# A hand-ordered attention and FFN kernel: the work of the first two blocks put in another order, q and k of the first pair loaded in halves by two queues

## The chip, the cores and the metric

One core of a Trainium2 chip. The time is the device time of one execution in microseconds (us). An interval of three runs stands beside the median where there is one.

## What is computed

Eight batches ("blocks" here) of linear attention with 8 heads, 576 rows and 64 columns each, and then one FFN over all 4608 rows, in float32:

```python
q_s = exp(q - max(q, axis=-1)); q_s = q_s / (sum(q_s, axis=-1) + 1e-9)      # per row
k_s = exp(k - max(k, axis=2));  k_s = k_s / (sum(k_s, axis=2) + 1e-9)       # per column, over 576 rows
kv  = einsum('bhsd,bhse->bhde', k_s, v)
x   = einsum('bhsd,bhde->bhse', q_s, kv)  ->  (4608, 512)
out = (relu(x @ w_in) ** 2) @ w_out       # w_in 512x2048, w_out 2048x512
```

## The kernel before, in words

**Tiles.** The eight heads of a block are taken as four pairs (`pr` 0 to 3); a pair fills 128 partitions. 512 of the 576 rows of a block go through the FFN directly, the other 64 ("left") are kept in DRAM for later. The FFN of a block has 16 steps `n` (128 of the 2048 hidden columns each). A step has four parts `h{n}_{c}`, where `c` is the pair whose x it multiplies, then `relu`, `rm` (times itself), `ghi` and `glo` (split in a rounded high part and the rest), and four parts `o{n}_{t}` into four output banks. Each part is three TensorE matmuls of 128x512, since each float32 product is made of high times high, high times low and low times high.

**A pair.** For q: `qm` (row maxima, DVE), `qsub` (POOL), `qexp` (ACT), `qs` (sums, DVE), `qadd` (POOL), `rc` (reciprocal, DVE), `qmul` (POOL), then `qt4` and `qt1` (transposes on TensorE) and `cp`, `cps` (copies by ACT). For k: `kmax` (DVE), `T` (transpose on TensorE), `mc` (DVE), `spread` (TensorE), `ke` (subtract, DVE), `kexp` (ACT), `kv` (TensorE, needs v as well), `rs`, `rr` (DVE), `kvn` (ACT or DVE). Then `at` (TensorE, x of 512 rows), `xhi` (ACT), `xlo` (DVE), and `atl`, `left`, `XL` for the 64 rows. A name with two digits, `kmax03`, is block 0, pair 3.

**Weights.** Each 128-column chunk `i{n}` of w_in and each chunk `o{n}` of w_out comes raw in 512 KB (`Li0`, `Lo0`), and is turned into a high and a low part by seven units: `L` (transfer), `low`, `t` (ACT), `s1`, `s2` (DVE), `hi` (ACT), `lo` (POOL). This is done once, beside the first block.

**What sets the order.** `ORDER` (line 51) is a list of these units, written out; the loop at line 1237 calls them one by one. The class `InOrder` (line 279) chains every instruction of an engine to the one before it on that engine, so each of TensorE, DVE, ACT, POOL and the transfer queue SP works through the list in its order and stops at the first unit whose input is late. A number behind a colon is the TensorE bank. `Z3:2` is three filler matmuls into bank 2; at the very start `beat(BEATS, banks[0])` (line 395) puts 28 fillers on TensorE, in front of everything. `ORDER` covers blocks 0 and 1 of the attention, the conversion of all weights, the 16 FFN steps of block 0 and the first two of block 1 (n = 16, 17), and parts of block 2; from `LIST` (line 91) on another list is followed, which stays as it is.

**Loads.** `load(b, pr, n)` (line 401) brings k, q or v of a pair in two transfers, the lower 64 partitions (160 KB) and the upper 64 (128 KB), on SP. Two exceptions stand at line 406 and 410: `Lk00` brings the lower half of k on SP and the unit `Lk00b` the upper half on ACT's queue; `Lq00` brings both halves of q on ACT's queue. The unit `warm` is a tiny exponential on ACT, there to get ACT's function table loaded early. Two tiles `kt` and `qt` serve the even and odd pairs of block 1 and later, so `Lk10` writes the tile that `kmax00` and `ke00` read.

Of the kernel before, what the change touches and what calls it, by code (L numbers as in the profile page):

```python
# [66 lines left out]
o3_0 o3_1 o3_2 relu4 Lv12 qexp11 kmax20 kexp12 Lq12 XL01 relu5 XL02 s1i6 s2i6 hii6 loi6 h6_0:1 h6_1 h6_2 h6_3 Lk13
rm4 qs11 qadd11 to4 s1o4 s2o4 Lo5 ghi4 hio4 glo4 loo4 o4_3 o4_2 o4_0 o4_1 atl10:0 Li8 qm12 qsub12 ti7 rm5 ghi5
kv12:3 glo5 lowo5 s1i7 s2i7 hii7 loi7 kmax13 relu6 rm6 h7_0:1 to5 s1o5 lowi8 s2o5 qexp12 qs12 qadd12 h7_1 h7_2 h7_3
rc11 qmul11 left10 T13:0 hio5 ti8 s1i8 Lo6 lowo6 rs12 rr12 kvn12 s2i8 to6 s1o6 qt411:3 Li9 loo5 o5_0 Lv11 o5_1 relu7  # L70
rm7 s2o6 hii8 loi8 o5_3 kv11:1 mc13 ghi6 glo6 ti9 cp11 lowi9 Lo7 lowo7 spread13 hio6 loo6 h8_0:3 h8_1 h8_2 Li10 ke20
rs11 rr11 kvn11 s1i9 s2i9 rc12 qmul12 Lo8 lowo8 at11:1 Li13 Lo10 ke13 to7 s1o7 s2o7 hii9 xhi11 lowi10 o6_3 loi9
xlo11 qt111:0 cps11 ti10 s1i10 s2i10 o5_2 ghi7 lowo10 glo7 o6_0 atl11:0 left11 Li15 hio7 loo7 to8 s1o8 s2o8 Lo11
hii10 h8_3 relu8 o6_2 hio8 rm8 h9_0:1 h9_1 h9_2 h9_3 relu9 o6_1 Lk21 o7_3 lowi15 qt412:0 ghi8 Li11 lowi11 kmax21
kexp13 loo8 loi10 o7_0 cp12 ti11 s1i11 s2i11 rm9 qt112:3 cps12 Lo9 o7_1 Lq13 qm13 lowo9 to9 hii11 o7_2 s1o9 glo8
o8_3 Lo13 at12:0 xhi12 h10_0:3 h10_1 h10_2 h10_3 XL11 Lv13 loi11 h11_0:1 h11_1 xlo12 kv13:0 h11_2 ghi9 glo9 Lq20
h11_3 qsub13 lowo11 relu10 Lo14 Li14 s2o9 ti12 hio9 loo9 o9_3 o8_1 o9_1 rm10 atl12:3 qexp13 s1i12 s2i12 to10 s1o10
s2o10 hii12 loi12 relu11 Lo12 Lv20 lowi13 qs13 qadd13 ti13 kexp20 lowi14 Lo15 Lq21 o8_0 o9_0 s1i13 hio10 loo10 rs13
rr13 kvn13 s2i13 rm11 lowo14 Lv21 WA0 WA1 ko0 ko1 to11 o8_2 o9_2 ghi10 ghi11 h12_0:0 h12_1 h12_2 h12_3 rc13 qmul13
s1o11 s2o11 ti14 s1i14 qsub20 Lq22 hio11 lowo12 qt413:1 left12 XL10 glo10 o10_2 o10_3 Lk22 hii13 relu12 qt113:3  # L80
o10_1 lowo13 cps13 atl13:3 left13 XL13 rm12 kv20:0 s2i14 loo11 XL12 loi13 h13_0:3 h13_1 h13_2 h13_3 hii14 qexp20
# [1255 lines left out]
```

## Time and profile before

| | us |
|---|---|
| median of 3 runs (838.13 to 839.73) | 838.84 |
| the profiled execution's own time | 838.89 |
| its span in the trace | 837.1 |
| TensorE busy (matmuls) | 828.8 (99%) |
| DVE busy | 540.8 (65%) |
| ACT busy | 486.7 (58%) |
| POOL busy | 288.2 (34%) |

The span is what lies between the first and the last instruction; 1.8 us of the profiled execution lie around it. Matmuls are pipelined, so that a busy TensorE is not one that does useful work all the time: the fillers count as busy, and so does a matmul that stands in the pipeline while the next one waits. All instructions have line 290, since one helper issues them; they are told apart by the tiles they write and read. Times of day below are us from the start of the span.

### The profile page before, as it was taken

To read this page: it belongs to the slowest core of one execution; us is meant where nothing else is said; L and a number is where in the kernel's file an instruction comes from. 1 tells how busy PE (TensorE), PEld (TensorE's weight loads), DVE (VectorE), ACT (ScalarE), POOL (GpSimd) and SP (SyncE) were. 2 spreads that over 40 slices of the span, in tenths; PEclk is the share of its full clock that TensorE was granted. 3 is DMA by queue.
4 is the path that set the end of the run, shared out by engine and by line. 5 is a ranking of instruction groups with operands and counts; after the bars stand their busy time and mean duration, and the time that the engine had idled before them with its cause. 6 is when DMAs were issued, how large, how long until landed. Compare 5 with 4: busy or idle time off the path is not lost.

```text
span 837.1 us, 12969 instructions
## 1 busy us (share of the span) xinstructions
PE 828.8 (99%) x4286; PEld 678.2 (81%) x4286; DVE 540.8 (65%) x1098; ACT 486.7 (58%) x898; POOL 288.2 (34%) x269
## 2 busy tenths in 40 slices
...
GB/s 240 270 186 299 279 287 214 327 215 98 211 256 249 227 283 259 277 281 258 234 252 245 283 159 213 271 187 189 172 233 177 98 227 156 163 166 154 186 55 50
DMA packets 156594, 179.65 MB, mean 215 GB/s; under 512 B 51696, under 2 KB 120304, under 8 KB 156528
## 3 DMA queue, kind: packets, MB, share of 16 engines
...
## 4 chain that ended last, share of the span: by engine, by line
PE 90%; DVE 4%; DMA 2%; issue 1%; POOL 1%; ACT 1%; SPq 1%; DVEq 0%; POOLq 0%; ACTq 0%
PE bank L290 90%; DVE m L290 1%; DMA raw_o<-in_moe_w_out_dram 1%; DMA qt<-in_q_dram 1%; SPq L290 1%; DMA raw_i<-in_moe_w_in_dram 0%; POOL qs L290 0%; DVE qs L290 0%; DVE g_lo L290 0%; DVE w L290 0%; POOL qn L290 0%; DVE xf L290 0%; DVE bank L290 0%; DVE r L290 0%; DVE qm L290 0%
## 5 line engine op out<-in xcount | busy, mean ns | idle before, releaser
L290 PE MATMUL bank<-wp,g 128*128 128x512 f32 x648 | 160.7, 390 | 0.0
L290 PEld LDWEIGHTS bank<-wp,g 128*128 128x128 f32 x648 | 120.6, 188 | 24.9
L290 PE MATMUL bank<-x_hi,wi 128*128 128x512 f32 x384 | 131.3, 396 | 0.0
L290 PE MATMUL bank<-xh_T,wp 128*128 128x512 f32 x384 | 130.7, 390 | 0.0
L290 PE MATMUL bank<-wo,g_hi 128*128 128x512 f32 x384 | 120.3, 394 | 0.0
L290 PE MATMUL bank<-xh_B,wp 128*128 128x512 f32 x288 | 98.0, 390 | 0.0
L290 POOL TENSOR_TENSOR qs<-qT,qs 64x640 fp32r<-64x640 f32 (+1 forms) x40 | 64.2, 1604 | 94.4 <-ACT qs L290 63.1
L290 DVE TENSOR_TENSOR c<-c,bank 128x512 f32<-128x512 f32 x48 | 32.9, 686 | 86.7 <-ACT c L290 86.4
L290 PEld LDWEIGHTS bank<-xh_T,wp 128*128 128x128 f32 x384 | 72.1, 188 | 16.3 <-ACT bank L290 1.2
L290 PEld LDWEIGHTS bank<-x_hi,wi 128*128 128x128 f32 x384 | 72.2, 188 | 15.9 <-DVE x_lo L290 0.4
L290 ACT ACTIVATE far<-far 128x512 f32<-128x512 f32 x96 | 60.6, 632 | 41.1 <-DVE far L290 39.9
L290 PEld LDWEIGHTS bank<-wo,g_hi 128*128 128x128 f32 x384 | 70.5, 188 | 14.8 <-ACT g_hi L290 0.4
L290 PE MATMUL bank<-wo,g_lo 128*128 128x512 f32 x192 | 75.0, 391 | 0.0
L290 PE MATMUL bank<-x_lo,wi 128*128 128x512 f32 x192 | 74.9, 390 | 0.0
L290 PE MATMUL bank<-xl_T,wp 128*128 128x512 f32 x192 | 74.8, 389 | 0.0
L290 PE MATMUL bank<-wo_back,g 128*128 128x512 f32 x288 | 71.4, 389 | 0.0
L290 DVE TENSOR_TENSOR g<-far,g 128x512 fp32r<-128x512 f32 x48 | 35.7, 781 | 43.5 <-ACT g L290 43.4
L290 DVE TENSOR_TENSOR far<-far,bank 128x512 f32<-128x512 f32 x48 | 32.9, 685 | 47.7 <-PE bank L290 47.5
L290 PEld LDWEIGHTS bank<-xh_B,wp 128*128 128x128 f32 x288 | 54.1, 188 | 11.6
L290 PEld LDWEIGHTS bank<-wo_back,g 128*128 128x128 f32 x288 | 53.6, 188 | 11.0
L290 POOL TENSOR_TENSOR qn<-qn,qs 128x640 f32<-128x640 f32 x30 | 37.8, 1261 | 69.6 <-DVE qs L290 47.0
L290 ACT CAST g<-far 128x512 fp32r<-128x512 f32 x48 | 27.5, 619 | 49.7 <-PE bank L290 49.4
...
## 6 DMA issues: line engine op xcount, KB each, us to landing
...
out_dram<-o SPq DMA_DIRECT2D x68, 128.0 KB, 2.9
...
```

What stands on the lines that cost most here:

```text
L290: ins = f(*args, **kwargs)
```

## The change

Two things. In `load`, q and k of block 0, pair 0 are both brought in halves: the lower on SP (`Lq00`, `Lk00`), the upper on ACT's queue (new unit `Lq00b`, and `Lk00b` as before). And `ORDER` is another arrangement of the same units (732 before, the one new unit besides), with the same banks and the same fillers; q of pairs 0 and 1 comes first, `Lk00b` now stands behind `warm`, and v of pair 1 comes before k of pair 2. `LIST` and all units stay the same.

```diff
 ORDER = """
-Lk00 Lq00 Lk00b warm qm00 qsub00 Lq01 qexp00 qm01 kmax00 qs00 Lk01 Li0 kmax01 T01:0 qsub01 qexp01 qadd00 rc00 Lk02
-Lq02 qs01 qadd01 Lq03 T00:1 mc00 mc01 Z3:2 spread01 rc01 kmax02 ti0 lowi0 s1i0 Li1 Lv01 ke01 kexp01 Z4:2 T02:2
-qmul01 qt101:3 Lk03 qm02 spread00 qt401:4 cps01 mc02 Lv00 qm03 Li2 qmul00 qt400:5 cp00 qt100:6 Z5:0 kv01:0 s2i0 ti1
-Lv02 ke00 Lk10 cps00 spread02 qsub03 qexp03 kmax03 lowi1 qsub02 qexp02 Z3:3 T03:3 qs03 rs01 rr01 kexp00 mc03 Lv03
-Li3 cp01 Z3:5 kv00:5 Lq10 spread03 kvn01 at01:1 atl01:6 qadd03 rc03 qmul03 qt403:4 lowi2 qs02 qadd02 rs00 rr00 kvn00
-ke02 kexp02 rc02 qmul02 hii0 cp03 atl00:0 ke03 kexp03 s1i1 s2i1 ti2 padv00 kmax10 qt103:5 cps03 at00:2 Lo0 hii1 loi1
-kv02:3 rs02 rr02 kvn02 xhi00 qt402:4 kv03:5 cp02 at02:3 Li4 T10:4 s1i2 xlo00 xhi01 rs03 rr03 kvn03 h1_0:2 xlo01
-xhi02 loi0 mc10 s2i2 at03:1 left00 lowi3 Lo1 qm10 ti3 xlo02 xhi03 lowo0 qt102:5 hii2 Lk11 Lv10 qsub10 s1i3 s2i3 hii3
...
-kvn10 hii4 lowo2 spread11 ke11 h3_3 to2 at10:2 loi4 h4_0:0 Li12 ghi0 kmax12 qt110:6 hio0 left02 T12:4 mc12 relu3
...
-h15_0:3 h15_1 h15_2 h15_3 Lv22 WA2 WA3 ko2 ko3 ghi13 relu14 to14 s1o14 s2o14 to15 glo13 o13_3 o13_1 o13_2 hio14
-loo14 o13_0 s1o15 s2o15 hio15 rm14 ghi14 glo14 h16_0:1 relu15 rm15 ghi15 glo15 Bw20 Lk23 WA4 ko4 o14_3 qsub21 at13:3
-loo15 o15_3 xhi13 xlo13 o14_0 o15_0 B20 rs20 h16_1 rr20 qexp21 ev3 S3 qn21 ev0 S0 ko6 Bw21 h16_2 o14_1 o15_1 ev1
...
+Lq00 Lq00b Lq01 warm Lk00 Lk00b Lk01 Lv01 qm01 Lk02 qsub01 qm00 Li0 qexp01 kmax00 qsub00 Li1 Lq03 kmax01 qexp00 Lq02
+qs01 T01:0 T00:1 Z3:2 mc01 qadd01 qs00 Lk03 spread01 Z4:2 rc01 mc00 qadd00 ke01 qmul01 Lv00 rc00 ti0 kmax02 qmul00
+lowi0 kexp01 s1i0 T02:2 qt101:3 spread00 qt401:4 cps01 s2i0 Li2 qt400:5 mc02 ti1 qm03 Lv03 qt100:6 Z5:0 cps00 cp01
+ke00 qsub03 lowi1 Lv02 kv01:0 qm02 kexp00 kmax03 qsub02 qexp03 Lk10 spread02 Z3:3 cp00 qs03 padv01 T03:3 qexp02 Lo0
+Z3:5 mc03 qadd03 rs01 hii0 Li3 rr01 kv00:5 rc03 qs02 qmul03 kvn01 s1i1 lowi2 Lq10 spread03 at01:1 rs00 padv00 rr00
+ke02 loi0 kvn00 Li4 atl01:6 s2i1 qt403:4 kexp02 Li5 qadd02 ke03 atl00:0 qt103:5 ti2 at00:2 Lk11 rc02 kmax10 cp03
+qmul02 kv02:3 cps03 left00 kexp03 Lo1 s1i2 xhi00 qt402:4 s2i2 hii1 kv03:5 Lv10 rs02 cp02 rr02 loi1 kvn02 xhi01 xlo00
+at02:3 lowi3 rs03 rr03 xlo01 ti3 T10:4 h1_0:2 qm10 hii2 h1_1 mc10 kvn03 s1i3 loi2 spread10 xhi02 at03:1 s2i3 lowi4
+xlo02 Lo2 qt102:5 hii3 h0_0:0 qsub10 ke10 xhi03 h1_2 cps02 xlo03 kexp10 loi3 h2_0:3 Li6 lowo0 h0_1 kmax11 Lk12 to0
...
+rr10 h3_1 s2i4 late cp10 glo1 mc11 h3_2 kvn10 hii4 kmax12 h3_3 to2 loi4 left02 spread11 hio1 o0_3:5 s1o2 relu3 qt110:6
+loo1 qm11 at10:2 lowi6 ke11 lowi12 h4_0:0 qsub11 s2o2 xhi10 o1_3 kexp11 xlo10 T12:4 h4_1 hio2 mc12 rm3 spread12 ti5
...
+qexp21 glo13 h15_0:3 hio13 XL13 rm14 h15_1 to14 loo13 Lk22 kf20 ghi14 h15_2 s1o14 kh20 h15_3 s2o14 o13_1 kl20 hio14
+Lq23 o13_3 relu15 loo14 to15 o13_2 rm15 Bw20 s1o15 o13_0 XL12 at13:3 s2o15 ko4 ghi15 glo14 hio15 h16_0:1 B20 xhi13
+loo15 h16_1 glo15 o14_3 xlo13 o15_3 Lv22 h16_2 ev3 o14_1 qn21 h16_3 qh20 o15_1 ko6 o14_0 S3 relu16 ql20 o15_0 rm16
...
 """.split()
@@ -403,13 +403,12 @@
-        if (b, pr, n) == (0, 0, 0):
-            units["Lk00b"] = lambda: e.act.dma_start(dst[HALF:, :, :HIGH, :], hi)
+        if (b, pr) == (0, 0) and n < 2:
+            units[f"L{'kq'[n]}00b"] = lambda: e.act.dma_start(dst[HALF:, :, :HIGH, :], hi)
             e.sp.dma_start(dst[:HALF], lo)
         elif n < 2 or b == 0:
-            on = e.act if (b, pr, n) == (0, 0, 1) else e.sp
-            on.dma_start(dst[:HALF], lo)
-            on.dma_start(dst[HALF:, :, :HIGH, :], hi)
+            e.sp.dma_start(dst[:HALF], lo)
+            e.sp.dma_start(dst[HALF:, :, :HIGH, :], hi)
```

## Rows read from the trace of the kernel before

**Rows 1.** Page: the chain that ended last, shares by engine.
```profile
PE 90%; DVE 4%; DMA 2%; issue 1%; POOL 1%; ACT 1%; SPq 1%; DVEq 0%; POOLq 0%; ACTq 0%
```

**Rows 2.** Chain of waits in order of time: start, length, what was waited for.
```profile
46.79 80.29 PE bank L290 x426
...
127.14 0.68 DVE r L290
...
194.58 637.71 PE bank L290 x3178
```

**Rows 3.** Timeline, TensorE: start, length, operation, count; fillers, first transpose, first FFN matmul, then at03.
```profile
1.31 9.39 PE L290 MATMUL bank<-x_hi 128*128 128x512 f32 x28 [1.31 <-POOL x_hi L290]
...
11.49 0.41 PE L290 MATMUL bank<-ident,m 128*128 128x128 f32 x2 [0.80 <-DVE qs L290]
...
29.53 0.50 PE L290 MATMUL bank<-x_hi,wi 128*128 128x512 f32 x1
...
30.55 1.12 PE L290 MATMUL bank<-qe,kvn 128*128 128x512 f32 x2
```

**Rows 4.** Waits by engine, 29.5 to 138 us: TensorE's weight loads (us, times, longest).
```profile
PEld bank L290 <- DVE mc L290: 0.8, 2, 0.5
PEld bank L290 <- DVE g_lo L290: 0.7, 2, 0.4
...
PEld bank L290 <- DVE m L290: 0.5, 1, 0.5
PEld bank L290 <- DVE r L290: 0.4, 1, 0.4
PEld bank L290 <- ACT g_hi L290: 0.4, 1, 0.4
```

**Rows 5.** Timeline from the start: the first transfers on both queues, ACT and DVE.
```profile
0.73 1.41 ACTq L290 DMA_DIRECT2D qt<-in_q_dram  x2
...
1.55 1.52 SPq L290 DMA_DIRECT2D qt<-in_q_dram  x2
...
2.17 0.62 ACTq L290 DMA_DIRECT2D kt<-in_k_dram  x1
...
2.82 1.28 ACT L290 ACT_TABLE_LOAD   x1 [2.82 <-issue]
...
4.12 0.20 ACT L290 ACTIVATE mc<-ones 128x1 f32<-128x1 f32 x1
...
6.18 0.82 DVE L290 TENSOR_REDUCE qm<-qt 128x10 f32<-128x640 f32 x1 [3.25 <-DMA qt<-in_q_dram]
```

**Rows 6.** Busy time by stretch: PE, PEld, DVE, ACT, POOL, clock, DMA share, GB/s.
```profile
5.00:10.00 5.00, 5.00 (x19) 4.03 (x18) 3.46 (x4) 1.15 (x2) 2.48 (x2) 1.00 1.09 274
```

**Rows 7.** Transfers issued before 30 us: count, KB each, median us from issue to landing.
```profile
qt<-in_q_dram ACTq DMA_DIRECT2D x1, 160.0 KB, 3.1
...
kt<-in_k_dram ACTq DMA_DIRECT2D x1, 128.0 KB, 4.5
```

**Rows 8.** Groups on DVE from 5 to 29 us: count, busy us, mean ns of one, idle before.
```profile
L290 DVE TENSOR_REDUCE m<-kt 128x128 f32<-128x640 f32 x5 | 6.5, 1299 | 0.0
L290 DVE TENSOR_REDUCE qm<-qt 128x10 f32<-128x640 f32 x4 | 3.3, 814 | 3.6 <-DMA qt<-in_q_dram 3.6
L290 DVE TENSOR_TENSOR ke<-kt,bank 128x640 f32<-128x640 f32 x4 | 3.2, 796 | 0.0
```

**Rows 9.** Timeline, DVE and SP: ke00, Lk10, kmax03, rs00, rr02, s2i2 and xlo00.
```profile
17.41 0.81 DVE L290 TENSOR_TENSOR ke<-kt,bank 128x640 f32<-128x640 f32 x1
18.14 1.30 DVE L290 TENSOR_REDUCE m<-kt 128x128 f32<-128x640 f32 x1
18.25 1.25 SPq L290 DMA_DIRECT2D kt<-in_k_dram  x2
...
22.43 0.16 DVE L290 TENSOR_SCALAR rs<-bank 128x1 f32<-128x1 f32 x1 [1.00 <-PE bank L290]
...
27.24 0.16 DVE L290 RECIPROCAL rs<-rs 128x1 f32<-128x1 f32 x1 [0.28 <-DVE rs L290]
...
28.78 0.69 DVE L290 TENSOR_TENSOR x_lo<-bank,x_hi 128x512 fp32r<-128x512 f32 x1
...
30.44 0.68 DVE L290 SCALAR_TENSOR_TENSOR w<-raw_i,bank 128x512 uint32<-128x512 uint32 x1
```

**Rows 10.** Timeline, POOL: the low part of o1.
```profile
42.39 1.30 POOL L290 TENSOR_TENSOR wo<-w,wo 128x512 fp32r<-128x512 f32 x1 [1.22 <-ACT wo L290]
```

More of the change, by code (lines that the diff above doesn't have):

```diff
@@ L57 @@
-ke02 kexp02 rc02 qmul02 hii0 cp03 atl00:0 ke03 kexp03 s1i1 s2i1 ti2 padv00 kmax10 qt103:5 cps03 at00:2 Lo0 hii1 loi1
-kv02:3 rs02 rr02 kvn02 xhi00 qt402:4 kv03:5 cp02 at02:3 Li4 T10:4 s1i2 xlo00 xhi01 rs03 rr03 kvn03 h1_0:2 xlo01
-xhi02 loi0 mc10 s2i2 at03:1 left00 lowi3 Lo1 qm10 ti3 xlo02 xhi03 lowo0 qt102:5 hii2 Lk11 Lv10 qsub10 s1i3 s2i3 hii3
-xlo03 spread10 ke10 loi2 qexp10 Lo2 h0_0:0 h0_1 qs10 cps02 h1_1 h1_2 h1_3 loi3 Li5 h0_2 to0 s1o0 lowo1 h2_0:3 h2_1
-h2_2 relu1 h3_0:1 kexp10 Lk12 qadd10 rc10 qmul10 lowi4 left01 s2o0 to1 rm1 h0_3 ghi1 glo1 h2_3 kmax11 atl03:4 s1o1
@@ L62 @@
-s2o1 padv01 Lo3 ti4 s1i4 left03 hio1 atl02:5 qt410:2 kv10:6 cp10 s2i4 loo1 rs10 rr10 T11:4 h3_1 mc11 h3_2 relu0 rm0
-kvn10 hii4 lowo2 spread11 ke11 h3_3 to2 at10:2 loi4 h4_0:0 Li12 ghi0 kmax12 qt110:6 hio0 left02 T12:4 mc12 relu3
-h4_1 h4_2 h4_3 loo0 kexp11 Lq11 s1o2 spread12 s2o2 late xhi10 xlo10 lowi5 glo0 o0_3:5 o1_3 o0_0:2 o1_0 hio2 ti5 loo2
-ke12 o0_2:4 o1_2 relu2 s1i5 Li6 Lo4 s2i5 lowo3 to3 hii5 loi5 qm11 cps10 o0_1:6 o1_1 Lk20 qsub11 rm2 h5_0:3 h5_1 h5_2
-h5_3 s1o3 s2o3 XL03 lowi12 lowi6 ghi2 glo2 o2_3 o2_1 o2_2 o2_0 lowo4 rm3 ghi3 glo3 Li7 ti6 XL00 lowi7 hio3 loo3 o3_3
@@ L67 @@
[L67 to L81, printed above, removed]
@@ L87 @@
-qh20 ql20 kf20 h16_3 relu16 rm16 ghi16 S1 B21 glo16 o14_2 o15_2 ev2 S2 kh20 kl20 Lq23 h17_0:3 h17_1 h17_2 h17_3
+Lq00 Lq00b Lq01 warm Lk00 Lk00b Lk01 Lv01 qm01 Lk02 qsub01 qm00 Li0 qexp01 kmax00 qsub00 Li1 Lq03 kmax01 qexp00 Lq02
+qs01 T01:0 T00:1 Z3:2 mc01 qadd01 qs00 Lk03 spread01 Z4:2 rc01 mc00 qadd00 ke01 qmul01 Lv00 rc00 ti0 kmax02 qmul00
+lowi0 kexp01 s1i0 T02:2 qt101:3 spread00 qt401:4 cps01 s2i0 Li2 qt400:5 mc02 ti1 qm03 Lv03 qt100:6 Z5:0 cps00 cp01
+ke00 qsub03 lowi1 Lv02 kv01:0 qm02 kexp00 kmax03 qsub02 qexp03 Lk10 spread02 Z3:3 cp00 qs03 padv01 T03:3 qexp02 Lo0
@@ new lines @@
+h0_2 left01 qexp10 h0_3 s1o0 lowi5 h3_0:1 qs10 lowo1 Lq11 h2_1 s2o0 qadd10 relu0 rc10 h2_2 qmul10 to1 rm0 Li12 h1_3
+hio0 s1o1 Lo3 h2_3 ghi0 loo0 s2o1 relu1 atl03:4 atl02:5 kv10:6 ti4 rm1 glo0 left03 s1i4 lowo2 qt410:2 rs10 ghi1 T11:4
+rr10 h3_1 s2i4 late cp10 glo1 mc11 h3_2 kvn10 hii4 kmax12 h3_3 to2 loi4 left02 spread11 hio1 o0_3:5 s1o2 relu3 qt110:6
+loo1 qm11 at10:2 lowi6 ke11 lowi12 h4_0:0 qsub11 s2o2 xhi10 o1_3 kexp11 xlo10 T12:4 h4_1 hio2 mc12 rm3 spread12 ti5
+loo2 h4_2 ke12 qexp11 o0_0:2 s1i5 cps10 Lk20 kexp12 o1_0 s2i5 lowo3 o0_1:6 qs11 Lo4 to3 o1_1 XL03 hii5 qadd11 s1o3
@@ new lines @@
+o0_2:4 relu2 Lv12 loi5 s2o3 h4_3 rm2 ti6 o1_2 kmax20 ghi2 h5_0:3 hio3 glo2 h5_1 XL00 ghi3 h5_2 Li7 lowo4 loo3 Lq12
+o2_1 relu4 rc11 s1i6 o2_2 glo3 Li8 s2i6 h5_3 Lk13 rm4 o2_0 to4 qmul11 relu5 o3_1 s1o4 Lo5 hii6 o3_2 s2o4 XL01 lowi7
+loi6 o3_0 rm5 Lv11 ti7 o2_3 qm12 hio4 o3_3 s1i7 ghi4 loo4 h6_0:1 s2i7 ghi5 h6_1 lowi8 glo4 Lo6 h6_2 hii7 kmax13 Li9
+h6_3 glo5 Lo7 o4_3 relu6 o4_0 qsub12 rm6 lowo5 o4_1 Li15 to5 o4_2 loi7 Lo10 qexp12 s1o5 kv12:3 Li10 ghi6 s2o5 XL02
+qs12 glo6 h7_0:1 hio5 Li13 lowo6 rs12 h7_1 rr12 Lo8 ke20 ti8 atl10:0 Lo11 h7_2 loo5 kvn12 s1i8 h7_3 kexp20 s2i8
```

16 lines of the change are left out of this document (14 added, 2 removed).

## The prediction, made before the changed kernel was run

> **What bounds the kernel now.** I read the page's chain first: 90% of it is TensorE [rows 1]. Then the chain in order of time: from 46.79 us it is TensorE nearly without a break, 80.29 us, one DVE step of 0.68 us at 127.14, TensorE again, and from 194.58 to the end TensorE alone [rows 2]. So after some 47 us a microsecond taken from any other engine is worth nothing unless TensorE stood still for it, and everything behind the reordered part should simply shift by what TensorE gains in it. What TensorE can gain is of three kinds. In the head it does fillers, transposes and small products until the first FFN matmul starts at 29.53 [rows 3]. The fillers and the waits make most of that time, though the page calls the engine 99% busy. Between 29.5 and 138 us its weight loads wait for DVE in a few places: for the column maxima (`mc`, `m`) 0.8 + 0.5 us, for `glo`, `rm` and `ghi` 0.7 + 0.4 + 0.4 us [rows 4]. The rest of that stretch is dense. The new order can therefore win a few microseconds of 838.89 at the very most, and only by an earlier first FFN matmul or by moving these waits.
>
> **The head: arrivals.** Before, DVE does its first reduction at 6.18, having waited 3.25 us for q of pair 0 [rows 5]. The changed kernel asks for q first: lower half of pair 0 on SP and upper half on ACT, both at 0.73, pair 1 on SP right behind. A first transfer took 3.1 us to land on the idle queues [rows 7], and the stream moves 274 GB/s [rows 6], which gives about 1.1 us for a 288 KB pair and 2.0 us for a 512 KB chunk (estimates from that row). q00 then lands near 4.4, and q01, whose second half is issued near 2.4 (SP's two took 1.52 us from 1.55 [rows 5]) and needs 3.1 more, at 5.5. DVE's first unit is now `qm01`: start 5.5, 0.7 earlier.
>
> k00's upper half is moved past `warm` on ACT. Before, ACT issued it at 2.17 and loaded its table after that, 1.28 us from 2.82 [rows 5]. Now the table load starts near 1.5, and the issue comes near 2.8, behind it. That is later by 0.6 us, but behind q it costs nothing: k00 would land at 6.6 by the stream, k01 at 7.8, and `kmax00` is due on DVE at 5.5 + two `qm` of 0.75 = 7.0. Should the 4.5 us that this transfer took before [rows 7] count from 2.8, it would be 7.3, a loss of 0.3 that the fillers below swallow. In the table's row the tiny exponential follows at 4.12, 0.02 us after the load. The Trainium skill ("ScalarE: Activation LUTs", section "What ACT_TABLE_LOAD costs") adds about 1.38 us of drain to a load of 1.28. By that rule the issue would come at 4.2 and k00 near 8.7, which leaves `mc01` 0.8 us later and the sum below 0.8 us smaller; the row shows no such drain.
>
> Behind k01 the stream holds, in the new order, v01 8.9, k02 10.0, i0 12.0, i1 14.0, q03 15.1, q02 16.2, k03 17.3, v00 18.4, i2 20.4, v03 21.5, v02 22.6, k10 23.7, o0 25.7, i3 27.7.
>
> **The head: DVE.** From 5.5: `qm01`, `qm00`, `kmax00` 7.0, `kmax01` 8.2, `qs01` 9.4 to 10.1. Here the gain is cut: `mc01` needs the transpose `T01`, and TensorE is in its 28 fillers until 10.7 [rows 3], which the change leaves alone. So `T01` runs at 10.7 instead of 11.49 and `mc01` at 11.0. An operation on DVE costs the queue some 0.08 us less than its row lasts: `ke00` lasts 0.81, and `kmax03` starts 0.73 behind its start [rows 9]. So from `mc01` to `kmax03` there are `kmax02` at 1.22, two `qm` and two `ke` at 0.73 [rows 8], `qs00` taken like a `qm`, `s1i0` and `s2i0` at 0.60 (0.68 for such a row [rows 9]), and five small ones that I take at 0.18 each: 1.2 + 5 x 0.73 + 1.2 + 0.9 = 6.95. All inputs above land in time, so `kmax03` starts at 17.9, against 18.14 [rows 9]. Two thirds of the early start are gone.
>
> From `kmax03` to `xlo00`, the last input of the first FFN part, it took 10.64 us (18.14 to 28.78). In it DVE stood 1.00 us for `rs00`, behind `kv00` on TensorE, and 0.28 for `rr02` [rows 9]. Now `s1i1` and others stand ahead of both, which gives the products time; I take both waits as gone. One more operation, `s2i2` of 0.68 us (0.6 by spacing), is pulled ahead of `xlo00`. So 10.64 - 1.28 + 0.60 = 9.96, and `xlo00` starts at 27.9, 0.9 us earlier.
>
> **The head: TensorE.** The first FFN part starts at 28.6 instead of 29.53. ACT has `lowi3` and `ti3` (which wait for i3 at 27.7) ahead of `kvn03`, so `at03` comes at 30.75, 0.2 later than at 30.55 [rows 3]; but `h1_1` is done by then, a part of three matmuls, 0.68 us. I book 0.8 us of gain, between 0.5 and 1.1.
>
> **From 32 to 50 us.** `spread11` moves behind `h3_3`, `T12` behind `o1_3`: of the waits for `mc` and `m`, 1.3 us in all [rows 4], about 0.7 is saved (a weight load runs ahead of its matmul, so not all of its wait is TensorE's). What is late next is `loo1` on POOL, 1.30 us a piece [rows 10], since `o1_3` is now asked for near 46 and not near 50: ACT's conversions `hio0`, `hii4`, `hio1` end near 39.5, 44 and 45.3 by my count, so `loo1` ends at 46.6. That costs about 0.4. Net gain 0.3, between -0.6 and 0.9.
>
> **From 120 to 130 us.** `rm15` stood behind `s2o15` and `glo14`; it was late for `at13`, which needs its bank, and `glo15` was late for `o15_3`: the 1.5 us of waits for `glo`, `rm`, `ghi` [rows 4], of which about 0.6 is TensorE's own. The new order puts `rm15` in front of `s1o15`, and `glo14`, `glo15` one or two parts ahead of their users. `kl20` is now in front of `rm15`, 1.5 us of DVE, but `at13` comes four parts after `h15_3`, 2.7 us. Gain 0.6, between 0 and 0.8.
>
> **The rest.** SP's queue carries the same transfers; `Lk10` still stops it until `ke00` is done (ke00 ran 17.41 to 18.22, `Lk10` issued at 18.25 [rows 9]), now near 17.2. POOL's q work keeps its order; `loi0` moves ahead of `qmul02` and delays it little, since `rc02` is due at 24. Each of the hundred moves in 50 to 120 us is covered by TensorE's dense work; if the cover is short somewhere, the price is a wait of 0.2 to 0.5 as in [rows 4]. I set 0.2 for new ones, between 0 and 1.5.
>
> **Sum.** 0.8 + 0.3 + 0.6 - 0.2 = 1.5 us off the profiled 838.89, 837.4. The median is 838.84, 0.05 away, so I keep 837.4. About 0.2% (1.7 us) is what a measurement of this kernel can tell from no change; the forecast lies just inside it.
>
> **Rivals.**
> 1. *More of it holds.* `loo1` is in time, `at03` is not held by i3, the gain of 0.9 at `xlo00` counts in full: 1.1 + 0.9 + 0.8 - 0 = 2.8, 836.1 us. For it: the order places each unit right behind its input. Against: ACT has hardly a gap from 22 to 46 in my count, so its small waits add up. Chance 0.2.
> 2. *The head is bound by arrivals and fillers anyway*, or ACT issues k00's half only behind the whole table load and the exponential (near 4.2, if the load itself starts only once `warm`'s input is ready, where I take 2.8): `xlo00` gains 0.1 or less, the middle nothing, the tail 0 to 0.6: 838.2 to 838.9. For it: DMA at a share of 1.09 [rows 6] and two thirds of the early start lost by 17.9. Chance 0.2.
> 3. *Slower.* i3 now stands behind v03, v02, k10 and o0 in the stream, and ACT waits for it in front of `hii2` and `kvn03`. i3 is needed by 27.4; each microsecond later holds `kvn03`, hence `at03`, hence all FFN parts behind it. `Lk10` holds SP for `ke00`: if `ke00` slips to 20, k10, o0 and i3 slip by 2.8 us too, i3 lands at 30.5, and `kmax10` on DVE is late as well. That costs 2.8 more in the head: 840.2 us. It decides from an `i3` later than 29.5, where the head's gain is gone. Against: `ke00` is two operations behind q03, which has 0.5 us to spare. Chance 0.15.
> 4. That the order doesn't reach the chip is excluded by the chains of `InOrder`, save for TensorE's records, which would show it.
>
> **How the numbers follow.** Forecast case 836.7 to 838.1, chance 0.45, about two fifths of it beyond 1.7 us of gain; with rival 1 that makes 0.38 faster. Rival 3 is slower, 0.15 with a little lost of it below the threshold and a little from unseen waits in the middle. Same: 0.47. The range for 8 in 10 goes from 835.8 (rival 1 with its best ends) to 839.5 (half of rival 3).
>
> **What would show it.** Right: first DVE reduction near 5.5, `T01` at 10.7 straight behind the fillers, `xlo00` near 27.9, first FFN matmul near 28.6, no TensorE wait for `rm` at 127, and the pure TensorE chain of the end starting near 193.1. Wrong: an ACT wait over 1 us for raw_i near 28, TensorE waiting for `loo` or `glo` between 45 and 60, or the head's gain given back before 100 us.

## The result, and the profile after

The changed kernel takes **848.37 us** (median of 4 runs, 846.63 to 848.88); the kernel before, beside it, 838.49 (4 runs, 838.1 to 839.73). The ratio is **1.0112, 95% interval 1.0093 to 1.0130**: 9.4 us slower, outside the range of the prediction and on the side that it gave 15%. The profiled execution of the changed kernel has a span of 846.6 us, 9.5 above that of before.

The page's chain after, shares by engine, to be set beside [rows 1]; and the last line of the chain in order of time, which answers to the last one of [rows 2]:

```profile
PE 82%; DVE 5%; DMA 5%; ACT 3%; SPq 2%; issue 2%; POOL 1%; DVEq 0%; POOLq 0%; ACTq 0%
```

```profile
203.94 637.88 PE bank L290 x3178
```

The stretch of TensorE alone at the end is as long as before (637.88 against 637.71) and begins 9.4 us later. So the whole loss lies ahead of 204 us. Of the chain ahead of that, some 56 us run over TensorE (82% of the span less the end), where some 116 did; transfers, DVE and ACT have taken its place. The timeline of TensorE, in the units of [rows 3] (fillers, `T01`, `T02`, `T03`, first FFN matmul, `at03`):

```profile
1.31 8.65 PE L290 MATMUL bank<-x_hi 128*128 128x512 f32 x28 [1.31 <-POOL x_hi L290]
10.12 0.41 PE L290 MATMUL bank<-ident,m 128*128 128x128 f32 x2 [0.16 <-DVE m L290]
13.91 0.33 PE L290 MATMUL bank<-ident,m 128*128 128x128 f32 x1 [1.53 <-DVE m L290]
21.98 0.33 PE L290 MATMUL bank<-ident,m 128*128 128x128 f32 x1 [2.75 <-DVE m L290]
...
34.50 0.47 PE L290 MATMUL bank<-x_hi,wi 128*128 128x512 f32 x1
...
36.19 1.02 PE L290 MATMUL bank<-qe,kvn 128*128 128x512 f32 x2
```

`T01` is 1.4 us earlier than before. `T03`, which ran at 19.53 before, is 2.5 us late, and the first FFN matmul 5.0 us. To follow the loss through the rest I take, for the later parts of each FFN step, TensorE's start less the full-clock lengths of the useful work that stands ahead of it in the order (0.68 us for an FFN part, no length for fillers). That is what TensorE has lost by then; "end of `ORDER`" is taken at the first matmul behind it, and the wait in `LIST` is the one for `kvs`, of which more below:

| lost, us | `T03` | step 1 | step 6 | step 8 | step 12 | end of `ORDER` | wait in `LIST` | span |
|---|---|---|---|---|---|---|---|---|
| before | 16.0 | 18.1 | 19.4 | 19.9 | 20.4 | 21.3 | 0 | 837.1 |
| after | 18.5 | 22.8 | 23.6 | 24.8 | 27.2 | 28.2 | 2.3 | 846.6 |

Three places make up the loss: **4.7 us in the head** (22.8 less 18.1), **2 us on the way to step 12**, and **2.3 us in the listed part**, where nothing was changed. The end of `ORDER` is 6.9 us late, and 6.9 + 2.3 is 9.2 of the 9.5.

**The head.** Its start went nearly as forecast (first reduction at 5.96, forecast 5.5). Timeline of ACT and its queue, to be set beside [rows 5]:

```profile
0.73 0.73 ACTq L290 DMA_DIRECT2D qt<-in_q_dram  x1
1.49 1.28 ACT L290 ACT_TABLE_LOAD   x1 [1.49 <-PEq L1320]
2.68 0.64 ACTq L290 DMA_DIRECT2D kt<-in_k_dram  x1
2.79 0.20 ACT L290 ACTIVATE mc<-ones 128x1 f32<-128x1 f32 x1
```

The upper half of k00 was issued at 2.68, before the table load was over, and the exponential came right behind the load. DVE and ACT afterwards (timeline; the last row is ACT's):

```profile
5.96 1.54 DVE L290 TENSOR_REDUCE qm<-qt 128x10 f32<-128x640 f32 x2 [3.03 <-DMA qt<-in_q_dram]
...
16.14 0.70 DVE L290 SCALAR_TENSOR_TENSOR bank<-bank,raw_i 128x512 uint32<-128x512 uint32 x1 [2.28 <-ACT raw_i L290]
...
18.47 0.82 DVE L290 TENSOR_REDUCE qm<-qt 128x10 f32<-128x640 f32 x1 [0.71 <-DMA qt<-in_q_dram]
...
20.67 1.25 DVE L290 TENSOR_REDUCE m<-kt 128x128 f32<-128x640 f32 x1
...
32.78 0.69 DVE L290 TENSOR_TENSOR x_lo<-bank,x_hi 128x512 fp32r<-128x512 f32 x1
```

```profile
14.88 0.65 ACT L290 ACTIVATE bank<-raw_i 128x512 f32<-128x512 f32 x1 [4.77 <-DMA raw_i<-in_moe_w_in_dram]
```

Both engines stand where a weight chunk is due in their order: ACT 4.77 us for i0 (`ti0`), and DVE 2.28 us behind it (`s1i0`). `kmax03` runs at 20.67 instead of 18.14 [rows 9]. The landing of a transfer in the trace is made of 16 counts, one from each DMA engine. When 14 of them and when all had come:

```
after   issued  14 of 16   all        before  issued  14 of 16   all
i0       7.68     12.34   14.85       i0       4.42      9.89   10.36
i1       8.32     14.40   17.67       i1       9.55     15.12   15.55
q03      8.87     15.07   18.17       q03      8.25     12.78   13.12
k03     11.83     17.58   19.48       k03     11.72     16.82   17.19
(q03 and k03: the lower half)
```

From i0 on the last count lags the fourteenth by 1.9 to 3.3 us, where before it was 0.3 to 0.5; the fifteenth lags it by 0.9 to 1.3. So one engine's share of the sixteen is late, and a second one by less. The Trainium skill says the same of the counts ("DMA: Bandwidth & Descriptors", section "Why a DMA increments its semaphore by 16 and not by 1"): the engines finish on their own, and only the full 16 mean that the data is there. In the three traces of kernels with i0 and i1 side by side (this one, e3 and e4) i0's last count lags by 1.8 to 2.5 us, in the other fifteen by 0.2 to 1.5, but for e8 with 2.5; whether the order brings the lag is not shown. SP is held by the late counts. Its queue (timeline):

```profile
7.68 1.14 SPq L290 DMA_DIRECT2D raw_i<-in_moe_w_in_dram  x2
...
11.83 1.26 SPq L290 DMA_DIRECT2D kt<-in_k_dram  x2
14.87 3.42 SPq L290 DMA_DIRECT2D vt<-in_v_dram  x2
18.33 1.10 SPq L290 DMA_DIRECT2D raw_i<-in_moe_w_in_dram  x1
```

The eighth transfer behind i0 is v00's first. It was issued at 14.87, when i0 had landed (14.85), its second half when i1 had (17.67). Before it was the same, v01 at 10.37 and i0 at 10.36, but there SP had been ready only just before. So in these traces eight transfers are in flight at most, and a lagging one stops the queue. Busy time by stretch, after and then before (columns as in [rows 6]):

```profile
15.00:20.00 5.00, 4.14 (x56) 3.10 (x53) 3.12 (x6) 3.65 (x8) 0.49 (x1) 1.00 0.62 148
20.00:25.00 5.00, 3.02 (x38) 2.39 (x40) 4.49 (x10) 4.40 (x8) 4.08 (x8) 0.76 0.99 247
25.00:30.00 5.00, 5.00 (x25) 3.59 (x23) 4.40 (x9) 2.75 (x8) 2.81 (x4) 0.55 1.07 301
```

```profile
15.00:20.00 5.00, 4.77 (x60) 3.77 (x59) 5.00 (x8) 3.80 (x8) 2.83 (x3) 1.00 1.11 274
20.00:25.00 5.00, 4.49 (x58) 3.14 (x56) 3.90 (x13) 4.71 (x11) 2.96 (x4) 1.00 0.81 217
25.00:30.00 5.00, 5.00 (x90) 3.78 (x90) 4.57 (x11) 3.83 (x9) 2.87 (x5) 1.00 1.00 326
```

From 15 to 20 us the stream moves 148 GB/s, where it moved 274. TensorE, which waited 1.53 and 2.75 us in front of `T02` and `T03`, then has a mean granted clock of 0.76 and 0.55: from 22.6 to 29.5 us it is at 0.50, the lower of its two levels (1.2 GHz). It does 25 instructions from 25 to 30 us where it did 90.

**On the way to step 12** the weight loads of TensorE wait for two things that they did not wait for before (waits by engine, 95 to 140 us):

```profile
PEld bank L290 <- POOL wo L290: 1.5, 2, 0.9
PEld bank L290 <- ACT bank L290: 1.3, 1, 1.3
```

The longer wait of the first row is `loo9`. The second stands in front of step 12; the row names ACT, but the bank is the one that `kvn13` on DVE reads until 108.25, and TensorE's weight load starts at 108.36. **In the listed part** (from `LIST` on) the waits of PE and DVE from 138 to 200 us, and then DVE's of before:

```profile
PE bank L290 <- DVE kvs L290: 2.3, 1, 2.3
...
DVE qm L290 <- DMA qt<-in_q_dram: 5.4, 1, 5.4
```

```profile
DVE qm L290 <- DMA qt<-in_q_dram: 3.0, 1, 3.0
```

DVE gets a q of block 3 2.4 us later in its own sequence, and passes that on to `kvs` and TensorE: TensorE's wait is DVE's less 3.1 us or so (5.4 and 2.3 here, 3.0 and none before, 4.6 and 1.5 in e3, 5.5 and 2.4 in e11). This lateness has two parts. SP issues that q later, as the experiments show below; and its last count came 1.2 us behind the fourteenth (179.74 and 178.51), with a packet of instructions (at 177.15, 0.96 us long) beside it. By the difference of 3.1 us this lag alone makes some 1.2 of the 2.3 us (an estimate). Seven of the eight runs with this wait have such a lag on that q, of 0.7 to 2.2 us, with such a packet beside it; in the eighth, e4, and in the ten runs without the wait it is 0.4 us at most.

### The profile page after: what moved, and what is told of

The parts are those of the page before. It is cut to its first block, busy times and chain, and to the rows that moved or that the text cites. A ratio compares the mean times of both kernels' runs of the same rounds, so it can differ in the third digit from the quotient of the medians.

```text
span 846.6 us, 12950 instructions
## 1 busy us (share of the span) xinstructions
PE 831.7 (98%) x4286; PEld 680.0 (80%) x4286; DVE 537.9 (64%) x1098; ACT 487.3 (58%) x898; POOL 288.0 (34%) x269
## 4 chain that ended last, share of the span: by engine, by line
PE 82%; DVE 5%; DMA 5%; ACT 3%; SPq 2%; issue 2%; POOL 1%; DVEq 0%; POOLq 0%; ACTq 0%
PE bank L290 82%; DMA raw_o<-in_moe_w_out_dram 2%; SPq L290 2%; DMA qt<-in_q_dram 2%; DVE bank L290 1%; DVE w L290 1%; DVE m L290 1%; ACT bank L290 1%; DVE qn L290 1%; DVE g_lo L290 0%; POOL qs L290 0%; DMA w_own<-wi 0%; ACT wo L290 0%; DVE ke L290 0%; DVE qm L290 0%
## 5 line engine op out<-in xcount | busy, mean ns | idle before, releaser
L290 PEld LDWEIGHTS bank<-wp,g 128*128 128x128 f32 x648 | 120.7, 188 | 24.8
L290 PE MATMUL bank<-x_hi,wi 128*128 128x512 f32 x384 | 133.5, 399 | 1.1 <-DVE kvn L290 0.9
L290 PEld LDWEIGHTS bank<-x_hi,wi 128*128 128x128 f32 x384 | 71.9, 188 | 18.6 <-ACT bank L290 1.3
```

The lines of the kernel that those rows point to most:

```text
L290: ins = f(*args, **kwargs)
```

## The experiments

All kernels are `ORDER`s made of the same units. Each ratio is to runs of the kernel before on the same chip at the same time. What TensorE lost (as in the table above), and the times:

| run | `T03` | step 1 | step 6 | step 8 | step 12 | end of `ORDER` | `LIST` | median us | ratio, 95% interval |
|---|---|---|---|---|---|---|---|---|---|
| e1 | 16.8 | 18.3 | 19.6 | 20.1 | 20.6 | 21.4 | 0 | 838.53 | 0.9995 (0.9978 to 1.0012) |
| e2 | 17.5 | 18.7 | 24.1 | 26.1 | 28.6 | 29.5 | 2.4 | 851.34 | 1.0146 (1.0122 to 1.0171) |
| e3 | 19.2 | 24.0 | 25.3 | 25.8 | 26.3 | 27.2 | 1.5 | 846.83 | 1.0093 (1.0070 to 1.0115) |
| e4 | 18.0 | 19.2 | 22.6 | 23.4 | 25.2 | 25.9 | 2.3 | 848.72 | 1.0122 (1.0097 to 1.0147) |
| e5 | 16.7 | 17.9 | 18.7 | 19.3 | 21.6 | 22.5 | 2.2 | 844.30 | 1.0064 (1.0043 to 1.0084) |
| e6 | 15.8 | 18.2 | 18.6 | 20.2 | 21.6 | 23.5 | 2.0 | 844.20 | 1.0063 (1.0038 to 1.0088) |
| e7 | 15.4 | 18.2 | 19.5 | 20.0 | 20.5 | 21.4 | 0 | 839.74 | 1.0006 (0.9995 to 1.0016) |
| e8 | 18.8 | 23.1 | 24.4 | 24.9 | 25.4 | 26.3 | 0 | 842.45 | 1.0036 (1.0023 to 1.0049) |
| e9 | 17.0 | 21.4 | 21.7 | 23.8 | 24.2 | 25.1 | 0 | 842.30 | 1.0034 (1.0017 to 1.0051) |
| e10 | 16.1 | 17.2 | 18.5 | 19.5 | 22.0 | 23.7 | 0 | 844.28 | 1.0058 (1.0037 to 1.0079) |
| e11 | 16.3 | 17.8 | 19.1 | 19.6 | 20.1 | 21.7 | 2.4 | 842.40 | 1.0037 (1.0024 to 1.0050) |
| e12 | 17.1 | 18.5 | 19.8 | 20.3 | 20.8 | 22.5 | 2.1 | 842.27 | 1.0040 (1.0023 to 1.0057) |
| e13 | 17.5 | 19.0 | 20.3 | 20.8 | 21.2 | 24.2 | 0 | 841.11 | 1.0024 (1.0014 to 1.0034) |
| e14 | 15.3 | 17.3 | 18.6 | 19.1 | 19.5 | 21.8 | 0 | 840.60 | 1.0022 (1.0011 to 1.0032) |
| e15 | 16.0 | 17.9 | 18.8 | 20.6 | 23.1 | 24.6 | 0 | 841.80 | 1.0035 (1.0022 to 1.0049) |
| e16 | 17.3 | 20.2 | 21.6 | 22.3 | 22.9 | 23.9 | 0 | 841.21 | 1.0029 (1.0016 to 1.0041) |

The columns of losses are one execution each, the times a median of 4 to 12. One kernel's runs scatter by 0.8 to 6.4 us (e10: 841.02, the profiled one, to 847.40), so the losses tell where time went and the ratios how much it is.

### The loads, the work and the transfers apart (e1 to e3)

e1 takes the new first loads into the old order:

```diff
-Lk00 Lq00 Lk00b warm qm00 qsub00 Lq01 qexp00
+Lq00 Lq00b Lq01 warm Lk00 Lk00b qm00 qsub00 qexp00
```

> The order of before, with only the first transfers changed: q of pair 0 in halves by SP and ACT, q of pair 1 behind it on SP, then k of pair 0. Theory A (the weights' chunks i0 and i1, taken back to back in front of q03, q02 and k03, make the head late): this part costs nothing, 837.8 to 838.8 us, first DVE reduction near 6.0 and first FFN matmul at 29 to 29.7. Rival D (the halves on two queues are what makes the stream late): 841 us or more, with q03 later than 16.

e2 keeps the changed order of the work and puts SP's first 31 transfers back in the old order, e3 is the reverse; the first of them, old and new:

```diff
-Li0 Lk02 Lq02 Lq03 Li1 Lv01 Lk03 Lv00 Li2
+Lv01 Lk02 Li0 Li1 Lq03 Lq02 Lk03 Lv00 Li2
```

> The changed order of all work of the engines, but SP's first 31 transfers in the order of before (i0, k02, q02, q03, i1, v01, k03). Theory A: most of the head's 5 us comes back: first FFN matmul at 30 to 31.5, granted clock 1.00 from 20 to 30 us, 843.5 to 845 us (the rest is lost behind 100 us). Rival B (the order of the work on ACT and DVE makes it late, whatever the transfers do): first FFN matmul at 34 or later, 847.5 to 849 us.

> The reverse: work in the order of before, SP's first 31 transfers in the order of the change. Theory A: the head is late by 3 to 5 us, 841.5 to 843.5 us, and nothing is lost behind 100 us. Rival B: 838 to 839.5 us.

**Measured.** e1 is the kernel before, 0.9995. Its timeline of DVE (first `qm`, and `kmax03`):

```profile
4.32 0.82 DVE L290 TENSOR_REDUCE qm<-qt 128x10 f32<-128x640 f32 x1 [1.40 <-DMA qt<-in_q_dram]
...
18.92 1.32 DVE L290 TENSOR_REDUCE m<-kt 128x128 f32<-128x640 f32 x1 [1.04 <-DMA kt<-in_k_dram]
```

DVE starts 1.9 us earlier than before and gives it all back in waits for transfers (0.67, 0.49, 0.62 and 1.04 us for q01, k00, k02 and k03): the halves are harmless and worth nothing, since the stream decides. The Trainium skill's advice against two transfers to disjoint halves of the partitions ("DMA: Bandwidth & Descriptors", section "Rules for kernel authors") agrees. e3 lost 5.9 us in the head and then ran parallel to before, step by step, up to the end of `ORDER`; its 846.83 lies above the range of theory A, with 1.5 us more in the listed part. So the order of the transfers alone makes the head late, and theory A holds for that. e2's head is whole (18.7), but its time missed every range: it lost 5 us between steps 1 and 6, where ACT waited 3.64 us for i5 (the granted clock was 0.50 from 45.5 to 48.9 us): the changed work wants i5 early, and its own transfers bring it early. I had not foreseen that.

### Which chunk, and what remains without it (e5, e6, e16)

e5 is the changed kernel with only the nine transfers of the last diff put back. e6 makes two more moves:

```diff
+hio9 loo9
 rc13 s2i12 lowo15 qmul13 h11_0:1
+rs13 rr13 kvn13
 qsub20
...
-hio9
...
-loo9
...
-rs13 rr13
...
-kvn13
```

> The changed kernel with nine transfers alone put back in the order of before (i0, k02, q02, q03, i1, v01, k03, v00, i2); the later ones, where the work of the changed kernel wants i5 early, stay as changed. Theory A (the head's 5 us come from i0 and i1 side by side ahead of q03, q02 and k03): first FFN matmul near 30.5, no gap at the fourth part's first matmuls as in the run with 31 transfers put back, 3 to 5 us above before (what is lost near 104 and 187 us). Rival B (the new order of the work is late by itself): 6 us or more above before.

> The same with two more moves: hio9 and loo9 ahead of rc13 and lowo15, and rs13, rr13 and kvn13 ahead of qsub20. If TensorE's waits at 104 to 108 us (0.71 for loo9, 1.05 for kvn13) are these two places of the order: both gone and 1.5 to 1.8 us less than with the nine transfers alone. If something behind them takes their place: the same time as there.

e16 is e3 with i1 taken out of the way (`ti1` and `lowi1` go behind `kexp00`):

```diff
-Lv01 Lk02 Li0 Li1 Lq03 Lq02 Lk03 Lv00 Li2
+Lv01 Lk02 Li0 Lq03 Lq02 Lk03 Li1 Lv00 Li2
```

> The order of before for the work and the changed order for the transfers, as in the run of that kind, but i1 behind k03 (and ti1 and lowi1 behind kexp00, so that ACT doesn't wait for it). If i1 in front of q03, q02 and k03 is what makes the head late: q03 lands near 15.5 (17.5 there), k03 near 17 (19.2 there), first FFN matmul at 30 to 31, 0.5 to 3 us above before. If i0's later place alone does it (ACT waited 4.57 us for it): first FFN matmul at 33 or later, 5 us or more above before.

**Measured.** Nine transfers take the whole kernel from 1.0112 to 1.0064, 4 us, and the head from 22.8 to 17.9; e5 is still 5.4 us above before, where theory A had 3 to 5. e16 went from e3's 1.0093 to 1.0029: i1 in front of q03, q02 and k03 is the larger part, 5.4 us, and i0's later place the rest. ACT still waits for i0 there:

```profile
13.88 0.63 ACT L290 ACTIVATE bank<-raw_i 128x512 f32<-128x512 f32 x1 [4.64 <-DMA raw_i<-in_moe_w_in_dram]
```

e6 removed the two waits at 99 to 104 us and won nothing, 1.0063 against 1.0064: step 12 now waits for the low part of a w_in chunk and `o10_3` for that of a w_out chunk (0.69 and 0.93 us lost). Mending one place shows the next.

### The clock (e4, e8)

e4 adds fillers to the changed kernel, e8 takes them out of e1:

```diff
-Z4:2
+Z11:2
...
-Z3:3
+Z13:3
```

> The changed kernel with 17 more filler matmuls (7 ahead of T02, 10 ahead of T03) in stretches where TensorE stood still for 2.7 and 3.7 us. Rival C (of the 5 us in the head some 2.8 are the granted clock of 0.76 and 0.55 between 20 and 30 us, which follows these two stops): clock 1.00 there, first FFN matmul near 32, 845 to 846.5 us. If the clock is not what the stops bring, or the work there waits for DVE and not for TensorE: 848 to 849 us.

> The order of before with the new first loads and without the 18 filler matmuls between 11 and 21 us (they compute nothing that is used). Theory C (the granted clock falls after TensorE stood still): clock below 1.00 somewhere from 15 to 30 us and 1.5 to 3 us above before. If the clock doesn't follow from it: the time of before or up to 0.5 us less.

**Measured.** e8 is 3.0 us above before (1.0036), although it only takes away work that nobody uses. Busy time by stretch in e8:

```profile
10.00:15.00 5.00, 1.80 (x9) 1.09 (x8) 3.59 (x9) 1.21 (x2) 2.72 (x3) 0.82 1.11 262
15.00:20.00 5.00, 3.23 (x27) 2.86 (x28) 3.65 (x6) 3.37 (x7) 2.46 (x2) 0.50 0.97 248
20.00:25.00 5.00, 5.00 (x76) 4.64 (x74) 3.54 (x10) 3.17 (x7) 1.76 (x4) 0.50 0.86 236
```

TensorE, busy 1.80 us of the five from 10 to 15, drops to half its clock from 13.2 to 30.2 us, and the first FFN matmul comes 4.8 us later than in e1 (34.55; the profiled run, 844.0, was the slowest of eight). Not all of that is the clock: in this execution i0's last count lagged by 2.5 us (1.2 in e1) and k03 was late with it, so that `kmax03` ran at 20.25, 1.3 us behind e1. No run separates the two. In e4 the clock is 1.00 throughout:

```profile
20.00:25.00 5.00, 4.97 (x57) 3.49 (x56) 4.93 (x13) 4.49 (x10) 4.04 (x9) 1.00 0.90 263
25.00:30.00 5.00, 4.96 (x97) 3.96 (x95) 4.85 (x11) 4.72 (x10) 3.42 (x4) 1.00 0.96 282
```

Its first FFN matmul comes at 30.91 and not 34.50, as theory C had it. But then ACT waits 1.41 us for i3 in front of `kvn03`, and DVE 1.16 for q10 in front of `mc10`; `at03` comes at 33.92, and by the end of `ORDER` 2.3 of the 3.6 us are left; the median (848.72) shows no gain at all. The clock is thus part of how the loss in the head comes about, not a cause that can be mended alone: a TensorE that is not slow meets the next late transfer. In e5 the wait in front of `T02` is there as well (1.54 us), but none in front of `T03`, and the clock stays at 1.00.

### k03 ahead of i1 in the old order (e7)

```diff
-Li0 Lk02 Lq02 Lq03 Li1 Lv01 Lk03 Lv00 Li2
+Li0 Lk02 Lq02 Lq03 Lv01 Lk03 Li1 Lv00 Li2
```

> The order of before with the new first loads, and v01 and k03 in front of i1 (ti1 and lowi1 behind kexp00, so that ACT doesn't wait for i1). With the new first loads alone DVE waited 1.04 us for k03. If the transfers' order sets the head: that wait gone, kmax03 near 17.5, first FFN matmul near 28.7, 0.5 to 1.5 us below before. If i1 is then late for ACT and DVE: 0 to 1 us above.

**Measured.** 1.0006. `T03` comes 1.4 us earlier than in e1, the first FFN matmul at 29.69 against 29.73: between the two DVE now waits twice 1.0 us, for `kv00` and for ACT. The transfer was the last to be late there, but not by much.

### How far the changed order can be kept (e9, e10)

Both are e5 up to a point and the old order behind it.

> The nine transfers in the order of before, the changed order of the work up to the first part of FFN step 6 (some 62 us), and from there the order of before. With the nine transfers put back the profile stood 0.7 us ahead of before at that point. Theory D (what is left of the loss comes from two later places of the new order: 1.8 us at 99 to 104, and some 2.2 us where TensorE waits for kvs near 180 us): 0 to 1 us below before, no wait over 0.3 us at the first product of pair 2 (near 178 us). Rival E (the later losses are the price of an earlier head, since transfers and conversions run in other company): 2 us or more above before.

> The same with the changed order up to FFN step 12 (some 103 us), the order of before behind it. Theory D: the waits for loo9 and kvn13 are there (0.7 and 1.0 us), the one for kvs near 180 us isn't; 1 to 2 us above before. If that one comes from the order before 103 us: 3.5 us or more above.

**Measured.** Neither has a wait for `kvs` in the listed part: with the old end of the order it is gone from the trace. In time both missed theory D. e10 has the two waits that were expected, but its median is 4.9 us above before, where 1 to 2 were expected and e5 has 5.4; its profiled run (841.02) is its fastest, and what the slower ones lost is in no trace. e9, at 2.9 us above, lies in rival E's range, but it lost 3.5 us in a head that was whole in e5, and only 0.5 more than before behind it; its runs lie between 839.36 and 845.11. Five kernels (e5, e6, e9, e10 and e15) have the same head, token for token. The row of `kmax10` in e9 and in e6 (timeline of DVE; in e5 and e10 it has no wait):

```profile
27.03 1.30 DVE L290 TENSOR_REDUCE m<-kt 128x128 f32<-128x640 f32 x1 [1.66 <-DMA kt<-in_k_dram]
```

```profile
25.26 1.29 DVE L290 TENSOR_REDUCE m<-kt 128x128 f32<-128x640 f32 x1 [1.10 <-DMA kt<-in_k_dram]
```

First FFN matmul: 28.93 in e10, 29.63 in e5 and e15, 29.87 in e6, 32.59 in e9. The changed head is 0.6 us better than before where the transfers come as counted, and 3 us worse in e9, where one count lags: those of k10 came from 23.68 to 26.94 in e9, from 22.98 to 24.71 in e5, and `kmax10` now stands in front of what `kvn` of pair 2 needs. That makes 2 of the 3 us (`kmax10` ran at 25.07 in e5). The third came on TensorE. Its timeline in e9, where this product has 1.10 us in e5:

```profile
30.69 2.04 PE L290 MATMUL bank<-qT,kvn 128*128 128x512 f32 x2 [1.62 <-DVE kvn L290]
```

The granted clock was 0.50 from 30.2 to 33.6 us there, the lower level, and 1.00 in e5 and e6. As to the late count: a packet of instructions ran at 22.17 us for 1.24 us, and from the next transfer on one count lags by 1.3 us or more, where it was 0.6 at most until then; in e6, with such a packet at 21.1 us, it is the same. The old head with the new loads (e1, e11 to e14) gave 28.73 to 30.41.

### The wait in the listed part (e11 to e15)

e11 is the old order up to step 12, with the changed one behind it. e12 moves one unit in it, e13 the last output parts, e14 takes the old order from step 16 on:

```diff
 ko6 o14_0 S3
+Bw21
...
```

```diff
-relu16 ql20 o15_0 rm16 h17_0:3 ghi16 h17_1 ev0 glo16 h17_2 S0 ev1 o14_2 o15_2 Bw21 h17_3 ev2 S1 B21 S2
+ql20 o15_0 ev0 S0 ev1 Bw21 o14_2 o15_2 ev2 S1 relu16 rm16 h17_0:3 ghi16 h17_1 glo16 h17_2 B21 h17_3 S2
```

> The reverse: the order of before, with the new first loads, up to FFN step 12, the changed order behind it. Theory D: nothing lost up to 138 us (0.3 us won for rm at 127 us), then 1.5 to 2.5 us of waiting for kvs near 180 us, since SP comes later to the listed part's first loads; 1.5 to 2.5 us above before. Rival E: no such wait, 0 to 0.5 us below before.

> The run before this one (order of before up to FFN step 12, changed order behind it) with one move: Bw21 in front of S0 in SP's queue. There SP stood from 134 to 138.7 us for ev0, with Bw21 ready at 134.8 behind it, so Bw21, B21, S2 and the listed part's first q loads all came some 4 us later. If that is what makes kvs late near 180 us: Bw21 near 135, first q load near 143, the wait for kvs 0.5 us or less instead of 2.4, and 1.5 to 2.5 us less than the run before, 0 to 1.5 us above the kernel before. If not: the same wait, 3 to 4 us above.

> The order of before up to FFN step 12 and the changed order behind it, but in the last 16 tokens of TensorE's, ACT's and SP's order o14_2, o15_2 and ev0 to ev2 stand ahead of step 17, so that S0, Bw21, S1 and B21 are no longer held by outputs that are late. If SP's lateness at the hand-over to the listed part makes kvs late: listed part's first q load near 143.5, no wait over 0.5 us for kvs, 1.5 to 2.5 us less than the run without this move. If the wait stays, SP isn't its cause.

> The same kernel with everything from step 16 on in the order of before. If the cause lies in the last 12 us of the order: no wait for kvs, 839.5 to 841 us. If it lies between 103 and 126 us: the wait of 2.4 us is still there, 842 us.

**Measured.** e11 has the wait (2.4 us) and 1.0037, without any change in the head. SP's queue in e11, and then in e14:

```profile
132.91 6.88 SPq L290 DMA_DIRECT2D out_dram<-o  x4
139.89 0.53 SPq L290 DMA_DIRECT2D bounce<-tb  x1
...
146.84 1.36 SPq L290 DMA_DIRECT2D qt<-in_q_dram  x2
```

```profile
131.16 2.46 SPq L290 DMA_DIRECT2D out_dram<-o  x4
...
134.35 0.40 SPq L290 DMA_DIRECT2D bounce<-tb  x1
...
141.26 1.36 SPq L290 DMA_DIRECT2D qt<-in_q_dram  x2
```

Four stores of finished outputs take SP 6.88 us instead of 2.46, since two of them (`S0`) wait for `ev0`, whose output part the new order puts behind step 16. The listed part's first q goes out 5.6 us later, while TensorE's `ORDER` ends within 0.2 us of the other. e12 missed: `Bw21` came 3.2 us earlier, but `B21` and `S2` still stood behind `S0`, and the first q left at 146.58. With the parts themselves ahead (e13: first q at 143.75) and with the old end (e14) the wait for `kvs` is 0. In time e14 is 1.3 us below e11 by the ratios (1.0022 against 1.0037), e13 1.1, with intervals that overlap; e13 pays for its own arrangement with one wait right behind step 17, which the table has at the end of `ORDER`:

```profile
PE bank L290 <- DVE g_lo L290: 1.1, 1, 1.1
```

So an SP that is late at 146 us is what TensorE meets at 180, 35 us on; with SP in time, that q has landed (at 167.58 in e14) ahead of the packet of instructions (169.18); in e11 the packet comes at 170.36 and the q at 173.48. The ratios show about half of the 2.4 us; the profiled run of e14 was its fastest.

e15 is the whole changed kernel with both corrections, the nine transfers and the last parts:

> The whole changed kernel with the nine transfers in the order of before and the last parts ahead. If the loss of the change is the place of the weights' chunks (4 us), the last parts (2 us) and the waits at 99 to 104 us (1.8 us), two of the three are gone: 1.5 to 3.5 us above before.

**Measured.** 1.0035, as expected: 6.5 of the 9.4 us are found in these two places. What is left, 2.9 us, is what the trace shows between steps 6 and 12 (18.8 to 23.1, against 19.4 to 20.4 before). No kernel was faster than before beyond its interval; e1 is the equal of it.

## Why the prediction was wrong, step by step

- **Arrivals.** This is the step that failed, and it made 4.7 of the 9.4 us. The stream was counted rightly: I had i0 at 12.0, i1 at 14.0, q03 at 15.1, k03 at 17.3, and 14 of the 16 counts had come for i0 by 12.34, for i1 by 14.40, for the lower half of q03 by 15.07 and for that of k03 by 17.58. But a transfer has landed with its last count: 14.85, 17.67, 18.17, 19.48. An order that leaves a transfer 0.5 us ("q03, which has 0.5 us to spare") has no room for that. In the old one q03 had landed 2.5 us ahead of its `qm` (13.57 and 16.09), and k03, which had 0.5, is the one that DVE waited for in e1.
- **"All inputs above land in time, so `kmax03` starts at 17.9."** It started at 20.67, behind the two units that waited for i0 and the `qm` that waited for q03. Up to `kmax02` (12.66) my count held: first reduction 5.96 (5.5), `T01` 10.12 (10.7).
- **The queue behind the waiting unit.** I counted SP's transfers as one stream and did not ask what issues them: with two chunks of 512 KB side by side and eight transfers in flight at most, SP stood still for 1.8 and then 2.2 us and the stream halved.
- **TensorE's clock** was not in the sum. I treated a wait of TensorE as worth its own length; two waits of 1.53 and 2.75 us were followed by clocks of 0.76 and 0.55 over 5 us each, which is 7 us at half clock. e8, whose trace has 17 us at half clock and k03 late besides, is 3.0 us above before; the price of the clock alone is not shown.
- **k00's half behind the table load.** The value I took (issue near 2.8) was right, 2.68. The Trainium skill's drain behind a table load ("ScalarE: Activation LUTs", section "What ACT_TABLE_LOAD costs") did not show: the exponential began 0.02 us after the load's end.
- **32 to 50 us: +0.3.** About right. In e5, where the head is whole, TensorE loses 0.8 us between steps 1 and 6, against 1.3 before.
- **120 to 130 us: +0.6.** The wait for `rm` is gone, and the gain is 0.2: from `h15_3` to the end of `ORDER` TensorE takes 15.68 us for the same matmuls, 15.91 before. A wait of 0.6 us for a low part of w_out is new there.
- **"0.2 for new waits, between 0 and 1.5."** It was 1.8 us at 104 to 108 and 2.3 in the listed part. Together that is 4 of the 9.4 us. The second came from a place that I had not looked at: I followed the end of the order on TensorE and DVE (`rm15`, `at13`) and not on SP's queue, past which the late output parts were moved.
- **Rival 3** had the kind right, a late transfer that holds an engine whose order puts it in front, and the wrong place and size: i0 and i1, not i3, and 9.4 us, not 1.4. Its own place shows in e4 (ACT 1.41 us for i3, in front of `kvn03`) and, through k10 and `kmax10`, in e9.

What stays open: what makes i0's last count lag. For k10 and the q of block 3 a packet of instructions beside them is the likely cause, but no trace has one between 0 and 17.9 us, and i0 has landed by then. And e14, whose profile equals that of e1, has runs 2 us slower in the median, and e10 runs up to 6 us slower than its trace.
